# Sharing early-batch work with ScalarE, moving stores to GpSimd, and three smaller schedule edits in a fused attention-and-mixer kernel

## The chip, the cores and the metric

One core of one Trainium2 chip. The metric is device time in microseconds (us) of one execution. TensorE is written PE in the profile, VectorE DVE, ScalarE ACT, GpSimd POOL, SyncE SP. To evacuate a PSUM buffer is to copy its contents to SBUF.

## The reference

Eight batches pass through a linear attention with 8 heads, then through a low-rank mixer and a two-layer network.

```python
q_p = concat(relu(q) * cos_w, relu(q) * sin_w)      # features, 8 x 8 x 576 x 128
k_p = concat(relu(k) * cos_w, relu(k) * sin_w)
kv  = einsum('bhsf,bhsd->bhfd', k_p, v);  z = sum(k_p, axis=2)
x   = (q_p @ kv) / (q_p . z + 1e-6)                 # reordered to 8 x 576 x 512
u   = x + (x^T @ U @ V)^T                           # rank 32
out = u + relu(u @ w_ch1) @ w_ch2                   # 512 -> 2048 -> 512
```

## The kernel before

The 576 rows of a batch are four chunks of 128 rows and a tail of 64. TensorE's order is a list of slots: for each pair of batches 16 slots with the first product of the even batch (`g_ps`, evacuated by ACT as `hid`), 16 of the odd batch, 4 of both tails (`gt_ps`), then 36 slots with a quarter each of a chunk's second product (`o_ps`). The attention of later batches is threaded between those slots by a plan of small units: a kv unit computes half of `kv` and `z`, an x unit one chunk of `x`, the A unit `x^T @ U`, a u unit one chunk of `u`. A k half is the cos or the sin half of one chunk's k features, one call of `scaled_relu`.

```python
def scaled_relu(eng, o, i, w):              # one half (cos or sin) of a feature
    if eng is nc.scalar:
        nc.scalar.activation(out=o, in_=i, func=AF.Relu, bias=0.0, scale=w)
    else:
        eng.tensor_scalar(out=o, in0=i, scalar1=0.0, scalar2=w, op0=ALU.max, op1=ALU.mult)

def g2_part(pr, cc, part):
    if part == 0:
        o_ps[pr, cc] = ps.tile([P, DM], FP32, tag="o", bufs=2, name="o_ps")
    # ... four of the chunk's 16 products, 512 columns each ...
    if part < 3:
        return
    o_sb = pool.tile([P, DM], FP32, tag="o_sb", bufs=3, name="o_sb")
    nc.vector.tensor_tensor(out=o_sb, in0=u, in1=o, op=ALU.add)
    nc.scalar.dma_start(out=..., in_=o_sb)  # the store sits in ACT's in-order queue

def attention_plan(b):                      # offsets in slots from the batch's base
    p0 = -18 if b % 2 == 0 and b > 2 else -14
    plan = [(p0, lambda: v_prep(b))]        # v casts, on GpSimd
    for n, c in enumerate(ORD):             # ORD = (4, 0, 1, 2, 3), 4 is the tail
        plan.append((p0 + n, lambda c=c: k_prep(b, c, (V_, V_))))
        # ... q features on ACT (batch 2: one half on DVE) ...
        plan.append((-9 + 2 * n, lambda c=c: qtr_unit(b, c)))   # q transposes
    # ... kv at 0 and 2; x units at 4, 6, .. 12; A at 14; u at 16 .. 20 ...

for b, w in ((2, 40), (3, 57), (4, 88), (5, 124), (6, 160), (7, 196)):
    ...                                     # the batch's plan at base slot w
```

The transposes, kv, A and u units share one PSUM buffer (tag `T`), the x units another (tag `X`). Both are filled by TensorE and must be emptied by DVE or ACT before they are filled again.

Of the kernel before, what the change touches and what calls it, by code (L numbers as in the profile page):

```python
# [13 lines left out]
ALU = mybir.AluOpType  # L14
# [3 lines left out]
def kernel(  # L18
# [11 lines left out]
    nc = tc.nc  # L30
# [7 lines left out]
    DM = 512  # L38
    DH = 2048
    R = 32  # L40
    NJ = DH // P
    NPAIR = B // 2
# [44 lines left out]
    w2_bf = const.tile([P, NJ, DM], BF16)  # L87
# [13 lines left out]
    def cast(eng, o, i):  # L101
# [6 lines left out]
    V_, A_, G_ = nc.vector, nc.scalar, nc.gpsimd  # L108
# [9 lines left out]
        out=iota[:, 0:4], pattern=[[1, 4]], base=0, channel_multiplier=4,  # L118
        allow_small_or_imprecise_dtypes=True,
    )  # L120
    for lo in (0, TS):
        nc.gpsimd.iota(
            out=iota[lo : lo + TS, 4:5], pattern=[[1, 1]], base=512, channel_multiplier=1,
            allow_small_or_imprecise_dtypes=True,
        )
    for h0 in (0, 4):
# [19 lines left out]
        out=stU[:, 0:4, :], in_=moe_U[0:512, :].rearrange("(p c) r -> p c r", c=4)  # L146
# [23 lines left out]
    def keep_warm(n, tag, bufs):  # L170
        w_ps = ps.tile([P, 512], FP32, tag=tag, bufs=bufs, name="w_ps")
        for _ in range(n):
            nc.tensor.matmul(out=w_ps, lhsT=zero[:, 0:P], rhs=zero, start=True, stop=True)
# [16 lines left out]
    u_bf, u_tl, uT, uT_tl = {}, {}, {}, {}  # L190
# [26 lines left out]
    def k_prep(b, c, engs, h0=0, h1=H):  # L217
        if b not in k_p:
            k_p[b] = pool.tile([P, 4, H, 2 * D], BF16, tag="k_p", bufs=1, name="k_p")
        src = kst[b][:, h0:h1, c, :] if c < 4 else kt[b][:, h0:h1, :]  # L220
        prep(k_p[b][:, c] if c < 4 else k_tl, src, b, c, engs, h0, h1)
# [7 lines left out]
    def kv_unit(b, hg, tag, bufs, eng=None):  # L229
        if b not in kv_sb:  # L230
            kv_sb[b] = pool.tile([P, H, E], BF16, tag="kv", bufs=2, name="kv")
        acc = ps.tile([P, 4, E], FP32, tag=tag, bufs=bufs, name="kv_ps")
        vx = v_ext[b % 2]
        for i in range(4):
            h = hg * 4 + i
            for c in range(5):
                nc.tensor.matmul(  # L237
                    out=acc[:, i, :],
                    lhsT=k_p[b][:, c, h, :] if c < 4 else k_tl[:, h, :],
                    rhs=vx[:, c, h, :],  # L240
                    start=(c == 0),
                    stop=(c == 4),
                )
        cast(eng or V_, kv_sb[b][:, hg * 4 : hg * 4 + 4, :], acc)
# [5 lines left out]
    def qtr_unit(b, c, h0=0, h1=H, eng=None, tag="T", bufs=1):  # L250
        qT_alloc(b)
        t_ps = ps.tile([P, H, P], BF16, tag=tag, bufs=bufs, name="t_ps")
        for h in range(h0, h1):
            nc.tensor.transpose(  # L254
                out=t_ps[:, h, :],
                in_=q_p[b][:, c, h, :] if c < 4 else q_tl[:, h, :],
                identity=ident,
            )
        if c < 4:
            cast(eng or V_, q_pT[b][:, c, h0:h1, :], t_ps[:, h0:h1, :])  # L260
        else:
            cast(eng or V_, q_tlT[:, h0:h1, tail(b)], t_ps[:, h0:h1, tail(b)])
# [161 lines left out]
    hid, hid_tl = {}, {}  # L424
# [37 lines left out]

    def g2_part(pr, cc, part):

        if part == 0:
            o_ps[pr, cc] = ps.tile([P, DM], FP32, tag="o", bufs=2, name="o_ps")
        o = o_ps[pr, cc]
        if cc == 4:
            lhs, c = hid_tl[pr], 0
        else:  # L470
            b, c = (2 * pr, cc) if cc < 4 else (2 * pr + 1, cc - 5)
            lhs = hid[b]
        for j in range(part * 4, part * 4 + 4):
            nc.tensor.matmul(  # L474
                out=o,
                lhsT=lhs[:, j, c * P : c * P + P],
                rhs=w2_bf[:, j, :],
                start=(j == 0),
                stop=(j == NJ - 1),
            )  # L480
        if part < 3:
            return
        o_sb = pool.tile([P, DM], FP32, tag="o_sb", bufs=3, name="o_sb")
        u = u_tl[pr] if cc == 4 else u_bf[b][:, c, :]
        nc.vector.tensor_tensor(out=o_sb, in0=u, in1=o, op=ALU.add)  # L485
        if cc == 4:
            for i in range(2):
                nc.scalar.dma_start(
                    out=out[2 * pr + i, 512:S, :], in_=o_sb[i * TS : i * TS + TS, :]
                )  # L490
        else:
            nc.scalar.dma_start(
                out=out[b, 0:512, :].rearrange("(p c) n -> p c n", c=4)[:, c, :], in_=o_sb
            )


# [18 lines left out]
    ORD = (4, 0, 1, 2, 3)  # L515

    def attention_plan(b):

        p0 = -18 if b % 2 == 0 and b > 2 else -14
        plan = [(p0, lambda: v_prep(b))]  # L520
        for n, c in enumerate(ORD):
            plan.append((p0 + n, lambda c=c: k_prep(b, c, (V_, V_))))
            if b == 2:
                plan.append((p0 + n, lambda c=c: q_prep(b, c, (V_, A_))))
            else:
                plan.append((p0 + n, lambda c=c: q_prep(b, c, (A_, None))))
                plan.append((p0 + n + 1, lambda c=c: q_prep(b, c, (None, A_))))
            plan.append((-9 + 2 * n, lambda c=c: qtr_unit(b, c)))
        plan.append((0, lambda: kv_unit(b, 0, "T", 1)))
        plan.append((2, lambda: kv_unit(b, 1, "T", 1)))  # L530
        for n, c in enumerate(ORD):
            plan.append((4 + 2 * n, lambda c=c: x_unit(b, c, "X", 1)))
        plan.append((14, lambda: A_unit(b, "T", 1)))
        for n, c in enumerate(ORD):
            plan.append((16 + n, lambda c=c: u_unit(b, c, "T", 1)))
        if b % 2 == 1:
            plan.append((18, lambda: utr_dma(b, 4, 5)))
        plan.append((19, lambda: utr_dma(b, 0, 2)))
        plan.append((21, lambda: utr_dma(b, 2, 4)))
        if b + 1 < B:  # L540
            for at, t in zip((p0 + 1, p0 + 2, p0 + 7), loads(b + 1, nc.sync)):
                plan.append((at, t))
        return plan


    l1 = loads(1, nc.sync)
    keep_warm(10, "X", 1)
    for c in ORD:
        k_prep(0, c, (V_, A_), 0, 4)
    l1[0]()  # L550
# [19 lines left out]
    keep_warm(3, "o", 2)  # L570
    for c in ORD[:2]:
        xh_unit(0, c, 0, 4, rec0, "o", 2)
    for n, c in enumerate(ORD):
        qtr_unit(0, c, 4, 8, (A_, A_, V_, A_, V_)[n], "g", 3)
    for c in ORD[2:]:
        xh_unit(0, c, 0, 4, rec0, "o", 2)
    kv_unit(0, 1, "T", 1)
    k_prep(1, 4, (V_, A_))
    uTd_open(0, 0, "g", 3)
    uTd_open(0, 1, "g", 3)  # L580
    rec1 = den_unit(0, 4, 8, "X", 1)
    k_prep(1, 0, (V_, A_))
    a0 = A_unit(0, "T", 1, A_, 0, 256)
    xh_unit(0, 4, 4, 8, rec1, "o", 2)
    xh_unit(0, 0, 4, 8, rec1, "o", 2)
# [2 lines left out]
    uTd_close(0, 1, A_)  # L588
    xh_unit(0, 2, 4, 8, rec1, "o", 2)
    xh_unit(0, 3, 4, 8, rec1, "o", 2)  # L590
    for c in (1, 2, 3):
        k_prep(1, c, (V_ if c == 1 else None, A_))
    uTd_open(0, 2, "g", 3)
    uTd_open(0, 3, "o", 2)
    A_unit(0, "T", 1, V_, 256, 512, a0)
    uTd_close(0, 2, V_)
    uTd_close(0, 3, A_)
    for c in (2, 3):
        k_prep(1, c, (V_, None))
    w1_load(2)  # L600
    v_prep(1, 0, 8, (4, 0, 1))
    w1_load(3)
# [9 lines left out]
    for n, c in enumerate(ORD):  # L612
        at((1, 2, 3, 4, 5)[n], lambda c=c: q_prep(1, c, (V_, A_)))
        ev = A_ if n in (0, 3) else V_
# [16 lines left out]
    for pr in range(NPAIR):  # L631
        e, o = 2 * pr, 2 * pr + 1
# [54 lines left out]
```

## Time and profile before

| | before |
|---|---|
| median of three runs | 356.58 us (356.54 to 357.55) |
| span of the profiled run | 355.6 us |
| PE busy, PE not busy | 327.5 us, 28 us |
| DVE, ACT, POOL busy | 169.1, 143.4, 37.1 us |

The lines that carry the argument stand in the prediction. Here are one group and one row of the DMA table from the page that it only uses in passing. Columns: line, engine, operation, output and input, shapes, count; then total busy us and mean ns of one; then the engine's idle time just before them and what ended most of it. The row below it gives KB of one store and the median us from issue to landing.

```profile
L431 PE MATMUL g_ps<-uT,w_bf 128*128 128x512 bf16 x512 | 121.2, 379 | 2.1 <-ACT hid L438 1.7
...
out_dram<-o_sb ACTq DMA_DIRECT2D x32, 256.0 KB, 2.4
```

TensorE waits for ACT's `hid` in the first product, and a store is in memory 2.4 us after ACT issues it. ACT's timeline (start, duration):

```profile
82.70 5.69 ACTq L492 DMA_DIRECT2D out_dram<-o_sb  x2
88.44 0.72 ACT L203 ACTIVATE q_tl<-qt,cosw 64x512 bf16<-64x512 f32 x1 [10.21 <-DMA out_dram<-o_sb]
```

The queue stood at two store issues for 5.69 us, since the second had to wait for its data. Batch 3's features came after them in the queue.

### The profile page before, as it was taken

How to read it: one execution, taken by the hardware profiler on the slowest of the kernel's cores; microseconds unless marked ns; L12 is line 12 of the kernel's file. 1: busy time of each engine (PE TensorE's matmuls, PEld its weight loads, DVE VectorE, ACT ScalarE, POOL GpSimd, SP SyncE). 2: the span in 40 equal slices, each digit the busy share in tenths (PEclk: the TensorE clock that was granted, in tenths of full speed). 3: DMA queues.
4: the chain of work that ended last, by engine and by line, in shares of the span. 5: the costliest groups of instructions: out<-in, count | busy, mean ns of one | idle time of the engine just before them, and what ended most of it. 6: DMA issues, size and time to landing. Idle time of an engine off the chain costs nothing.

```text
span 355.6 us, 6095 instructions
## 1 busy us (share of the span) xinstructions
PE 327.5 (92%) x2539; PEld 175.7 (49%) x2539; DVE 169.1 (48%) x362; ACT 143.4 (40%) x249; POOL 37.1 (10%) x71
## 2 busy tenths in 40 slices
PE   4669999999787988999999988999999999999995
PEld 1454664475443534556555534556555544464442
DVE  4775454764955685244744681244744640001121
ACT  1957745650600066555530048555530026760000
POOL 6340503030300012000003000300000000000000
PEclk9698999999999999999999999999999999999998
DMA  7999999969242775300896159500312150000221
GB/s 211 259 279 254 196 220 255 259 169 281 80 147 55 189 247 137 58 2 0 125 287 199 59 143 244 147 2 2 89 61 59 61 133 2 1 2 29 88 81 69
DMA packets 60172, 46.04 MB, mean 129 GB/s; under 512 B 26704, under 2 KB 55408, under 8 KB 60144
## 3 DMA queue, kind: packets, MB, share of 16 engines
q1 hardware_dynamic: 50400, 31.46, 36.2%
q0 software_dynamic: 4496, 4.74, 7.9%
q10 hardware_dynamic: 5248, 9.44, 7.7%
q8 instruction: 20, 0.33, 0.4%
q14 instruction: 8, 0.07, 0.1%
HBM read 36.86 MB, written 9.44 MB: 130 GB/s over the span
## 4 chain that ended last, share of the span: by engine, by line
PE 77%; DVE 8%; DMA 8%; ACT 2%; SPq 2%; issue 1%; POOL 1%; POOLq 0%; DVEq 0%; ACTq 0%
PE o_ps L474 31%; PE g_ps L431 28%; DMA kst<-in_k_dram 5%; PE t_ps L254 4%; PE gt_ps L449 4%; DMA vt<-in_v_dram 3%; PE va_ps L361 3%; PE a_ps L344 2%; PE kv_ps L237 2%; PE x_ps L318 2%; DVE k_p L205 2%; ACT q_p L203 1%; DVE o_sb L485 1%; SPq L75 1%; DVE u_bf L362 1%
## 5 line engine op out<-in xcount | busy, mean ns | idle before, releaser
L431 PE MATMUL g_ps<-uT,w_bf 128*128 128x512 bf16 x512 | 121.2, 379 | 2.1 <-ACT hid L438 1.7
L474 PE MATMUL o_ps<-w_bf,hid 128*128 128x512 bf16 x512 | 119.3, 379 | 0.0
L438 ACT ACTIVATE hid<-g_ps 128x512 bf16<-128x512 f32 x128 | 75.9, 596 | 77.8 <-PE g_ps L431 77.6
L431 PEld LDWEIGHTS <-w_bf 128*128 128x128 bf16 x512 | 48.0, 98 | 59.5 <-issue 10.1
L474 PEld LDWEIGHTS <-hid 128*128 128x128 bf16 x512 | 48.0, 98 | 52.2 <-issue 1.2
L485 DVE TENSOR_TENSOR o_sb<-u_bf,o_ps 128x512 f32<-128x512 bf16 x32 | 21.9, 684 | 61.9 <-PE o_ps L474 61.9
L105 POOL CAST v_ext<-vst 128x512 bf16<-128x512 f32 (+1 forms) x32 | 18.3, 610 | 169.1 <-DMA vst<-in_v_dram 140.8
L105 DVE COPY q_pT<-t_ps 128x1024 bf16<-128x1024 bf16 (+1 forms) x29 | 19.4, 671 | 30.0 <-PE t_ps L254 28.6
L203 ACT ACTIVATE q_tl<-qt,cosw 64x512 bf16<-64x512 f32 x5 | 3.6, 719 | 62.0 <-DVE rec L276 27.3
L362 DVE TENSOR_TENSOR u_bf<-x_bf,va_ps 128x512 bf16<-128x512 bf16 x32 | 21.9, 685 | 12.1 <-PE va_ps L361 12.0
L254 PE MATMUL t_ps<-ident,q_p 128*128 128x128 bf16 x256 | 20.6, 224 | 4.1 <-ACT q_tlT L103 1.0
L203 ACT ACTIVATE q_p<-qst,sinw 128x512 bf16<-128x512 f32 (+1 forms) x36 | 23.3, 664 | 2.4 <-DVE o_sb L485 2.3
L254 PEld LDWEIGHTS <-q_p 128*128 128x128 bf16 x256 | 17.4, 100 | 10.8 <-issue 5.0
L205 DVE TENSOR_SCALAR k_p<-kst,cosw 128x512 bf16<-128x512 f32 (+1 forms) x36 | 16.8, 482 | 2.8 <-DMA kst<-in_k_dram 2.7
L361 PE MATMUL va_ps<-A_sb,V_bf 128*128 128x512 bf16 x40 | 15.1, 377 | 2.8 <-DVE u_bf L362 2.4
L328 DVE TENSOR_TENSOR x_bf<-x_ps,rec 128x512 bf16<-128x512 f32 x24 | 16.6, 691 | 0.8
L449 PE MATMUL gt_ps<-uT_tl,w_bf 128*128 128x128 bf16 x256 | 16.1, 219 | 0.0
L449 PEld LDWEIGHTS <-w_bf 128*128 128x128 bf16 x256 | 15.1, 98 | 1.4
L474 PE MATMUL o_ps<-w_bf,hid_tl 128*128 128x512 bf16 x64 | 15.4, 379 | 0.0
L105 DVE CAST kv<-kv_ps 128x260 bf16<-128x260 f32 x16 | 6.9, 429 | 17.2 <-PE kv_ps L237 17.2
L237 PEld LDWEIGHTS <-k_p 128*128 128x128 bf16 x256 | 11.1, 99 | 7.8 <-DVE q_pT L105 2.5
L237 PE MATMUL kv_ps<-v_ext,k_p 128*128 128x65 bf16 x256 | 12.3, 195 | 2.5 <-DVE u_bf L362 1.9
(93 smaller groups left out, 254.0 us busy)
## 6 DMA issues: line engine op xcount, KB each, us to landing
out_dram<-o_sb ACTq DMA_DIRECT2D x32, 256.0 KB, 2.4
kst<-in_k_dram SPq DMA_DIRECT2D x7, 1024.0 KB, 11.2
qst<-in_q_dram SPq DMA_DIRECT2D x7, 1024.0 KB, 7.9
vst<-in_v_dram SPq DMA_DIRECT2D x7, 1024.0 KB, 11.1
w_bf<-in_moe_w_ch_dram POOLq DMA_DIRECT2D x8, 512.0 KB, 12.0
kst<-in_k_dram SPq DMA_DIRECT2D x2, 512.0 KB, 7.8
qst<-in_q_dram SPq DMA_DIRECT2D x2, 512.0 KB, 8.7
vst<-in_v_dram SPq DMA_DIRECT2D x2, 512.0 KB, 11.4
```

What stands on the lines that cost most here:

```text
L105: eng.tensor_copy(out=o, in_=i)
L203: nc.scalar.activation(out=o, in_=i, func=AF.Relu, bias=0.0, scale=w)
L205: eng.tensor_scalar(out=o, in0=i, scalar1=0.0, scalar2=w, op0=ALU.max, op1=ALU.mult)
L237: nc.tensor.matmul(out=acc[:, i, :], lhsT=k_p[b][:, c, h, :] if c < 4 else k_tl[:, h, :], rhs=vx[:, c, h, :], start=(c == 0), stop=(c == 4),)
L254: nc.tensor.transpose(out=t_ps[:, h, :], in_=q_p[b][:, c, h, :] if c < 4 else q_tl[:, h, :], identity=ident,)
L361: nc.tensor.matmul(out=va, lhsT=V_bf[:, c, :], rhs=A_sb[b], start=True, stop=True)
L362: nc.vector.tensor_tensor(out=u_bf[b][:, c, :] if c < 4 else u_tl[b // 2][rows, :], in0=x_of(b, c, rows), in1=va[rows, :], op=ALU.add,)
L431: nc.tensor.matmul(out=g_ps.rearrange("p (c t) -> p c t", c=4), lhsT=w1_bf[:, d, j * P : j * P + P], rhs=uT[b][:, :, d, :], start=(d == 0) ...
L438: nc.scalar.activation(out=hid[b][:, j, :], in_=g_ps, func=AF.Relu, bias=0.0, scale=1.0)
L449: nc.tensor.matmul(out=g_ps[:, jj, :], lhsT=w1_bf[:, d, j * P : j * P + P], rhs=uT_tl[pr][:, d, :], start=(d == 0), stop=(d == 3),)
L474: nc.tensor.matmul(out=o, lhsT=lhs[:, j, c * P : c * P + P], rhs=w2_bf[:, j, :], start=(j == 0), stop=(j == NJ - 1),)
L485: nc.vector.tensor_tensor(out=o_sb, in0=u, in1=o, op=ALU.add)
```

## The change

Five intents: work of batches 2 and 3 goes from DVE to ACT; the stores leave ACT's queue for GpSimd's (the last pair's go to SyncE's), so that ACT is free for that work; the features of batches 4 and 6 move eight slots earlier, out of the slots of the first product; the start is reordered so that batch 1's k features don't hold up batch 0's chain; the last chunk is computed in two column halves. In the core of the diff, cuts are marked:

```diff
 def g2_part(pr, cc, part):
+    last = pr == NPAIR - 1 and cc == 8
     ...
+    if last:      # first 256 columns, all 16 products; then the other 256
+        cols, js = slice(part // 2 * 256, part // 2 * 256 + 256), part % 2 * 8
+        js = range(js, js + 8)
     ...
-    nc.vector.tensor_tensor(out=o_sb, in0=u, in1=o, op=ALU.add)
+    nc.vector.tensor_tensor(out=o_sb[:, cols], in0=u[:, cols], in1=o[:, cols], op=ALU.add)
+    eng = nc.sync if pr == NPAIR - 1 else nc.gpsimd
-    nc.scalar.dma_start(...)
+    eng.dma_start(...)

 def attention_plan(b):
-    p0 = -18 if b % 2 == 0 and b > 2 else -14
+    p0 = -26 if b % 2 == 0 and b > 2 else -14
     for n, c in enumerate(ORD):
-        plan.append((p0 + n, lambda c=c: k_prep(b, c, (V_, V_))))
+        ke = (V_, A_) if b == 3 else (V_, V_)
+        plan.append((p0 + n, lambda c=c, ke=ke: k_prep(b, c, ke)))
     ...
-        plan.append((-9 + 2 * n, lambda c=c: qtr_unit(b, c)))
+        ev = A_ if b in (2, 3) and n % 2 == 0 else V_
+        plan.append((-9 + 2 * n, lambda c=c, ev=ev: qtr_unit(b, c, eng=ev)))

 # the start
-keep_warm(10, "X", 1)
+keep_warm(20, "X", 1)
 ...
+kv_unit(0, 1, "T", 1)          # between the third and fourth q transpose,
 ...                            # before: after the last x unit of the first half
-k_prep(1, 4, (V_, A_)); ...; k_prep(1, 0, (V_, A_))   # between uT, den and A of batch 0
 ...
+k_prep(1, 4, (None, A_)); k_prep(1, 0, (None, A_))    # only after batch 0's x units
 ...                            # and the other halves after its last uT
```

More of the change, by code (lines that the diff above doesn't have):

```diff
@@ L468, in g2_part @@
         if cc == 4:
-            lhs, c = hid_tl[pr], 0
+            b, lhs, c, u = None, hid_tl[pr], 0, u_tl[pr]
         else:
             b, c = (2 * pr, cc) if cc < 4 else (2 * pr + 1, cc - 5)
-            lhs = hid[b]
-        for j in range(part * 4, part * 4 + 4):
+            lhs, u = hid[b], u_bf[b][:, c, :]
+        if last:
+            cols, js = slice(part // 2 * 256, part // 2 * 256 + 256), part % 2 * 8
+            js = range(js, js + 8)
+        else:
+            cols, js = slice(0, DM), range(part * 4, part * 4 + 4)
+        for j in js:
             nc.tensor.matmul(
-                out=o,
+                out=o[:, cols],
                 lhsT=lhs[:, j, c * P : c * P + P],
-                rhs=w2_bf[:, j, :],
+                rhs=w2_bf[:, j, cols],
                 start=(j == 0),
@@ L480, in g2_part @@
             )
-        if part < 3:
+        if js[-1] < NJ - 1:
             return
         o_sb = pool.tile([P, DM], FP32, tag="o_sb", bufs=3, name="o_sb")
-        u = u_tl[pr] if cc == 4 else u_bf[b][:, c, :]
-        nc.vector.tensor_tensor(out=o_sb, in0=u, in1=o, op=ALU.add)
+        nc.vector.tensor_tensor(
+            out=o_sb[:, cols], in0=u[:, cols], in1=o[:, cols], op=ALU.add
+        )
+        eng = nc.sync if pr == NPAIR - 1 else nc.gpsimd
         if cc == 4:
             for i in range(2):
-                nc.scalar.dma_start(
+                eng.dma_start(
                     out=out[2 * pr + i, 512:S, :], in_=o_sb[i * TS : i * TS + TS, :]
@@ L491, in g2_part @@
         else:
-            nc.scalar.dma_start(
-                out=out[b, 0:512, :].rearrange("(p c) n -> p c n", c=4)[:, c, :], in_=o_sb
+            eng.dma_start(
+                out=out[b, 0:512, cols].rearrange("(p c) n -> p c n", c=4)[:, c, :],
+                in_=o_sb[:, cols],
             )
@@ L572 @@
         xh_unit(0, c, 0, 4, rec0, "o", 2)
-    for n, c in enumerate(ORD):
-        qtr_unit(0, c, 4, 8, (A_, A_, V_, A_, V_)[n], "g", 3)
+    for n, c in enumerate(ORD[:3]):
+        qtr_unit(0, c, 4, 8, (A_, A_, V_)[n], "g", 3)
+    kv_unit(0, 1, "T", 1)
+    for n, c in enumerate(ORD[3:]):
+        qtr_unit(0, c, 4, 8, (A_, V_)[n], "g", 3)
     for c in ORD[2:]:
         xh_unit(0, c, 0, 4, rec0, "o", 2)
-    kv_unit(0, 1, "T", 1)
-    k_prep(1, 4, (V_, A_))
     uTd_open(0, 0, "g", 3)
@@ L581 @@
     rec1 = den_unit(0, 4, 8, "X", 1)
-    k_prep(1, 0, (V_, A_))
     a0 = A_unit(0, "T", 1, A_, 0, 256)
@@ L590 @@
     xh_unit(0, 3, 4, 8, rec1, "o", 2)
-    for c in (1, 2, 3):
-        k_prep(1, c, (V_ if c == 1 else None, A_))
+    k_prep(1, 4, (None, A_))
+    k_prep(1, 0, (None, A_))
     uTd_open(0, 2, "g", 3)
@@ L597 @@
     uTd_close(0, 3, A_)
-    for c in (2, 3):
-        k_prep(1, c, (V_, None))
+    for c in ORD:
+        k_prep(1, c, (V_, None if c in (4, 0) else V_))
     w1_load(2)
```

## The prediction

> **What bounds the kernel now.** I read the engine shares first, then the chain that ended last, then ten-microsecond windows to see where TensorE is not full, then the timeline inside those windows.
>
> ```profile
> PE 327.5 (92%) x2539; PEld 175.7 (49%) x2539; DVE 169.1 (48%) x362; ACT 143.4 (40%) x249; POOL 37.1 (10%) x71
> ...
> PE 77%; DVE 8%; DMA 8%; ACT 2%; SPq 2%; issue 1%; POOL 1%; POOLq 0%; DVEq 0%; ACTq 0%
> ```
>
> TensorE is the bound, and no other engine is half full. No product is removed, so the change can win only from TensorE's gaps: 355.6 - 327.5 = 28 us. The windows say where these are (columns after the stretch: PE, PEld, DVE, ACT, POOL busy; then clock and DMA).
>
> ```profile
> core 0: us, PE busy (x) PEld busy (x) DVE busy (x) ACT busy (x) POOL busy (x), PEclk, DMA share, GB/s
> 0.00:10.00 10.00, 4.37 (x10) 1.34 (x10) 5.06 (x19) 2.81 (x6) 5.37 (x16) 0.94 0.81 206
> 10.00:20.00 10.00, 7.58 (x95) 5.74 (x96) 7.40 (x25) 10.00 (x26) 5.52 (x13) 0.72 1.12 281
> 20.00:30.00 10.00, 7.01 (x104) 5.16 (x102) 6.03 (x16) 5.22 (x9) 2.10 (x5) 0.83 1.18 249
> ...
> 90.00:100.00 10.00, 7.82 (x73) 4.25 (x73) 8.24 (x21) 4.91 (x8) 3.33 (x5) 1.00 0.28 85
> 100.00:110.00 10.00, 7.78 (x51) 3.87 (x50) 6.18 (x12) 0.00 (x0) 0.00 (x0) 1.00 0.37 118
> 110.00:120.00 10.00, 8.35 (x86) 4.67 (x87) 5.70 (x12) 0.00 (x0) 0.00 (x0) 1.00 0.37 79
> ...
> 130.00:140.00 10.00, 8.21 (x43) 3.71 (x42) 7.12 (x12) 8.36 (x15) 3.41 (x5) 1.00 0.35 79
> ...
> 210.00:220.00 10.00, 8.15 (x41) 3.65 (x41) 4.19 (x10) 9.40 (x17) 0.00 (x0) 1.00 1.06 255
> ```
>
> Idle TensorE: 11.0 us before 30 us, 6.05 us from 90 to 120 (ACT is empty from 100 to 120), 1.8 near 130, 1.85 near 210. The timeline names the releaser of each gap.
>
> ```profile
> 24.56 0.72 ACT L203 ACTIVATE k_p<-kst,sinw 128x512 bf16<-128x512 f32 x1 [1.83 <-DMA kst<-in_k_dram]
> ...
> 24.95 0.41 DVE L304 TENSOR_TENSOR x_tl<-xh_ps,rec 64x256 bf16<-64x256 f32 x1
> 25.19 0.36 ACT L103 ACTIVATE A_sb<-a_ps 128x256 bf16<-128x256 f32 x1
> ...
> 25.61 0.42 PE L402 MATMUL uT_ps<-V_bf,A_sb 128*128 128x512 bf16 x1 [1.65 <-ACT A_sb L103]
> ...
> 75.20 0.61 PE L254 MATMUL t_ps<-ident,q_p 128*128 128x128 bf16 x8 [0.80 <-DVE q_tlT L105]
> ...
> 96.77 0.43 PE L318 MATMUL x_ps<-kv,q_pT 128*128 128x65 bf16 x8 [1.40 <-DVE x_bf L328]
> ...
> 100.47 0.61 PE L254 MATMUL t_ps<-ident,q_p 128*128 128x128 bf16 x8 [0.78 <-DVE q_pT L105]
> ...
> 133.54 0.38 PE L361 MATMUL va_ps<-A_sb,V_bf 128*128 128x512 bf16 x1 [0.75 <-DVE u_bf L362]
> ...
> 215.09 1.02 PE L431 MATMUL g_ps<-uT,w_bf 128*128 128x512 bf16 x4 [0.68 <-ACT hid L438]
> ```
>
> Batch 1's k features sit in the in-order queues of ACT and DVE ahead of batch 0's evacuations, and its load lands only at 24.6. So x_tl and A_sb are late, and TensorE waits. Later the releaser is a backlog on DVE (75.20, 96.77, 133.54) or on ACT (215.09). A part of the gaps is different: at 100.47, 104.71, 108.03 and 110.57 TensorE waits 0.77 to 0.78 us, just one evacuation of 0.69 us plus some 0.1. There one PSUM buffer is filled, emptied and filled again with nothing between; a free engine doesn't shorten that.
>
> **What the Trainium skill says.** "ScalarE: Activation LUTs", section "What ACT_TABLE_LOAD costs": an ACTIVATE takes 186 ns + 0.833 ns an element with immediate operands, about 93 ns more for a pointer scale. The trace agrees: 596 ns for hid (512 elements), 710 for a q feature (pointer scale), 1.04 us for a q_pT copy of 1024. DVE copies q_pT in 0.69 us, so ACT is the slower evacuator.
> "VectorE: DVE Perf Modes", section "The perf-mode tier table (the rule you actually need)": an fp32 SBUF tensor_scalar runs at twice the basic rate, a tensor_tensor from PSUM at the basic one. The trace: 0.47 us for a k feature of 512 (0.395 from start to start), 0.69 for x_bf, u_bf and o_sb.
> "DMA: Bandwidth & Descriptors", section "SWDGE vs HWDGE vs iDMA": a DMA issued from GpSimd has its descriptors written in software. The trace has weight loads on POOL at 746 to 912 ns an issue, against 0.34 us for a store on ACT that finds its data ready. POOL is 90% idle.
> "TensorE: Matmul & The Clock Gate", section "What's actually happening": an idle window of some 3.4 us throttles the array to half rate, some 3.4 us of work releases it. The trace: after the idle stretch 5.56 to 11.43 us eight transposes take 0.86 us, later 0.44; after the gap ending 25.61 eight of them again spread over some 0.9.
>
> **The change part by part.**
>
> *Start.* (a) Ten more warm-up products: 10 x 0.43 = 4.3 us from 5.56, over at 9.9, before the first transpose at 11.43. They delay nothing; the first transposes run at full rate. But ACT is full from 10 to 20, so little of that arrives: -0.2. (b) Batch 1's k features leave the queue ahead of batch 0's chain. The second kv product moves up into a 0.59 us TensorE wait at 18.9 to 19.5. By hand along DVE: rec at 23.9 as now, x_tl then at once, at 23.95 instead of 24.95: -1.0. A_sb follows at 24.0 instead of 25.19, so the gap before 25.61 nearly closes and the array stays warm: eight transposes (0.86 to 0.44) and four half-width A products (0.86 to 0.5) save 0.8. First g product 28.5 instead of 30.48. (c) Does it stay? Batch 1's q lands at 32.5, which still allows the interleaved slots to begin 2 us earlier; v lands at 38.6, and the kv product moves from 41.6 to 39.7; the last quarter of w1 lands at 45.45, while its first use moves from 47.35 to 45.4. All three just hold. The start gives **-2.0**.
>
> *Batches 2 and 3.* q_tlT of batch 2 goes to ACT, so the 0.80 at 75.20 goes: **-0.8**. For batch 3, five k halves of 0.395 (2.0 us) and three evacuations (0.41 + 2 x 0.69 = 1.8 us) leave DVE, which is 82% busy from 90 to 100. Its backlog gaps 0.46 (92.76) and 1.40 (96.77) are 1.86; I leave 0.3. The structural 0.78s stay. On ACT the last evacuation is 1.04 instead of 0.69 ahead of a u product only four matmuls away: +0.35. Together 1.86 - 0.3 - 0.35 = **-1.2**. ACT carries it: without the stores ahead of them, batch 3's features start near 84 when their buffers are free (now 88.44, held 10.21 us behind a store), 15 x 0.62 = 9.3 us.
>
> *Features of batches 4 and 6 eight slots earlier*, out of the first product's slots, where ACT also evacuates hid: gaps of 0.35 + 0.75 + 0.69 = 1.8 for batch 4, and 0.74 + 0.37 + 0.68 + 0.68 = 2.5 for batch 6 vanish. But in the instruction order of the changed kernel the ten k halves now stand between the x_bf evacuations of the batch before. For batch 4: two slots are 1.98 us of TensorE; DVE must do in them one x unit (1.03), four k halves (1.58) and half an o_sb (0.30), 2.9. With one PSUM buffer for x, TensorE waits; stepping through the five slots I get 0.1 + 0.65 + 1.2 = 1.95. For batch 6 only the last two x units are concerned: 0.85 + 0.33 + 0.12 = 1.3. Net 4.3 - 3.25 = **-1.0**.
>
> *Stores on GpSimd:* 30 issues of about 0.75 us on an idle engine, hidden; they free ACT. *End:* now o_sb runs 351.55 to 352.24 and the span ends 3.3 us later. With halves the last add is some 0.41 instead of 0.69 (the 256-column x_bf takes 0.41), half of the 256 KB is out before, and 32 products of 256 columns cost perhaps 0.1 more than 16 of 512: **-0.4**.
>
> Sum: -2.0 - 0.8 - 1.2 - 1.0 - 0.4 = -5.4; 356.58 - 5.4 = **351.2 us**.
>
> **The rivals.**
> 1. *The moved features only move the stall.* For: the 2.9 against 1.98 us above. If GpSimd's v casts fall on the same time, k halves stretch as at 93 us now (0.83 to 0.92 against 0.47), ten of them by up to 0.4. Then batches 4 and 6 gain nothing or lose 1 to 2: 353 us.
> 2. *The start is bound by loads.* For: DMA is saturated (1.1 to 1.2) from 10 to 60 us. The last w1 quarter is issued on POOL behind batch 1's v casts, so its landing doesn't move up with TensorE. If a landing slips by 1 us, so does the gain: 352.5. Against: the three margins fit now, if barely.
> 3. *The store issue becomes the wait.* A store on GpSimd waits behind a v cast whose load is late; three output buffers fill, DVE waits, TensorE follows. For: v casts waited 140 us for loads. Against: in the new order each v load is issued well ahead of its cast. It would make 354 to 356.
> 4. *Fewer backlogs than I count.* If DVE has slack at batches 4 and 6 because k features spread into later slots, both gaps go: 349 us.
>
> **Range and chances.** The five terms are uncertain by about 0.8, 0.3, 0.7, 1.5 and 0.3 us, together near 1.9. Rivals 1 to 3 pull up, 4 pulls down. I take 349.0 to 353.8. Two per cent faster means below about 349.5: 17%. Within 2%: 82%. Slower by 2%: 1%, as no new work is on TensorE.
>
> **What would show it.** First g product near 28.5 us, with x_tl near 24; if it starts there but the first tail product (72.45 now) hasn't moved by 2 us, rival 2. No DVE-released gap of 1.4 between 90 and 98, but still three or four of 0.78 up to 115. No gaps with u_bf or hid as releaser in the first product of batches 2 and 4, and new ones, released by x_bf, in the second product before them (some 1.9 and 1.2 us); none there means rival 4, more means rival 1. POOL with about 30 issues near 0.75 us, and no wait of DVE for a store. I'd be wrong at the root if TensorE's total idle time fell by less than 2 us or by more than 8.

## The result, and the profile after

The kernel is correct. In the runs made together on one chip the changed kernel took 352.17 us (median of four, 352.06 to 352.83) and the kernel before 357.05 (median of four, 356.54 to 357.55). The ratio is 0.9867, with a 95% interval of 0.9845 to 0.989. A ratio here is the mean time of one kernel's fast runs over that of the other's of the same rounds, so not quite the ratio of the medians. This is a gain clear of the noise, but short of two per cent. 351.2 us had been predicted, with a range from 349.0 to 353.8. The span of the profiled run went from 355.6 to 350.3 us. The mean granted clock of the two profiles differs (0.983 and 0.994), but from 30 us on to the end of the work it is 1.00 in both; before that it is 0.83 and 0.94, which is a part of the start.

The changed kernel's page, with the same parts as shown of before: shares of the span, the chain, groups, landings.

```profile
PE 326.5 (93%) x2537; PEld 177.0 (51%) x2565; DVE 165.8 (47%) x355; ACT 150.5 (43%) x257; POOL 52.2 (15%) x101
...
PE 75%; DVE 9%; DMA 9%; issue 3%; POOL 2%; ACT 1%; SPq 0%; POOLq 0%; DVEq 0%
...
L431 PE MATMUL g_ps<-uT,w_bf 128*128 128x512 bf16 x512 | 120.6, 379 | 0.4
L491 DVE TENSOR_TENSOR o_sb<-u_bf,o_ps 128x512 f32<-128x512 bf16 (+1 forms) x33 | 22.1, 669 | 61.6 <-PE o_ps L481 61.6
L501 POOL DMA_DIRECT2D out_dram<-o_sb x24 | 13.4, 558 | 180.9 <-DVE o_sb L491 164.4
...
out_dram<-o_sb POOLq DMA_DIRECT2D x24, 256.0 KB, 4.5
out_dram<-o_sb SPq DMA_DIRECT2D x7, 256.0 KB, 2.3
```

TensorE's work is the same; 28 us of it not busy have become 24. The first product has almost no idle time left (2.1 to 0.4 us). A store issue costs GpSimd 0.56 us. It lands after 4.5 us instead of 2.4, but that is not the price of GpSimd alone: the experiments below give 3.0 with the stores alone on GpSimd and 3.0 with them back on ACT, and from 245 to 286 us, where few loads run, it is 2.4 here against 2.1 before. Nothing waits for it: all idle time of DVE before `o_sb` was ended by TensorE, none by a store.

Four windows of the changed kernel, ten microseconds each, with the columns that the prediction explains (the stretch, its length, then busy PE):

```profile
120.00:130.00 10.00, 8.94 (x55) 4.12 (x55) 6.63 (x15) 1.79 (x3) 2.67 (x5) 1.00 1.12 310
130.00:140.00 10.00, 10.00 (x65) 5.15 (x64) 3.89 (x7) 5.38 (x9) 1.32 (x3) 1.00 0.50 85
...
200.00:210.00 10.00, 8.83 (x40) 3.79 (x40) 6.47 (x12) 1.81 (x4) 3.85 (x7) 1.00 1.15 286
210.00:220.00 10.00, 10.00 (x69) 5.41 (x68) 1.81 (x3) 6.00 (x11) 0.13 (x1) 1.00 0.17 45
```

The holes that the prediction showed at 130 and 210 us are full, but there are new ones just before them. In the kernel before, the stretches just before were fuller:

```profile
120.00:130.00 10.00, 10.00 (x69) 4.76 (x67) 7.71 (x21) 2.17 (x4) 0.00 (x0) 1.00 0.98 305
...
200.00:210.00 10.00, 9.31 (x49) 4.06 (x46) 6.50 (x14) 0.90 (x2) 0.00 (x0) 1.00 0.28 81
```

**Where the 5.3 us are.** TensorE's products come in the same order in both kernels after the start. So I took the start of one and the same product in both traces, slot by slot (of its weight load, since some products are missing in the traces). Where the difference stays constant, nothing is won or lost; where it steps, the step is the gain or the loss of that place. The table's steps add up to the difference of the spans, -5.27 us.

| stretch | predicted | read in the two traces |
|---|---|---|
| start, up to the 13th first product of batch 0 | -2.0 | -3.37 at the first one, -2.66 left at the 13th |
| batch 2's `q_tlT` on ACT | -0.8 | -0.97 |
| rest of batches 2 and 3 | -1.2 | -0.56 |
| features of batch 4 eight slots earlier | +0.15 (1.95 - 1.8) | +0.17 (2.21 - 2.04) |
| features of batch 6 eight slots earlier | -1.2 (1.3 - 2.5) | -1.5 (1.47 - 2.97) |
| end | -0.4 | +0.25 |
| sum | -5.4 (rounded) | -5.27 |

These are three of TensorE's waits in the changed kernel's timeline (start, duration, work; in brackets the idle time before it and its releaser):

```profile
89.85 0.43 PE L318 MATMUL x_ps<-kv,q_pT 128*128 128x65 bf16 x8 [1.16 <-DVE x_bf L328]
...
123.18 0.43 PE L318 MATMUL x_ps<-kv,q_pT 128*128 128x65 bf16 x8 [1.06 <-DVE x_bf L328]
...
344.80 1.91 PE L481 MATMUL o_ps<-w_bf,hid 128*128 128x256 bf16 x16 [0.51 <-DVE o_sb L491]
```

The wait of 1.06 is the foreseen one of batch 4's features (with 0.18 and 0.46 before it). Those at 89.85 and 344.80 were not foreseen. For the first, GpSimd's and then DVE's timeline of the changed kernel show the cause:

```profile
84.87 0.56 POOL L501 DMA_DIRECT2D out_dram<-o_sb  x1 [4.96 <-DVE o_sb L491]
85.43 2.28 POOL L105 CAST v_ext<-vst 128x512 bf16<-128x512 f32 x4
```

```profile
86.16 2.60 DVE L205 TENSOR_SCALAR k_p<-kst,cosw 128x512 bf16<-128x512 f32 x2
```

Two k halves took 2.60 us. Four v casts of batch 3 ran on GpSimd at that time; in the queue they stand behind a store, which had waited 4.96 us for `o_sb`. In "SBUF — State Buffer", section "Who interferes with whom", the Trainium skill says that VectorE in a two-port mode and GpSimd share one pair of ports, and that whichever issues first blocks the other for its whole instruction. The trace agrees that they block each other: the same two halves take 0.86 us in a kernel where the casts lie elsewhere (the early-cast experiment below). The wait can be longer than one instruction, as the run with the stores alone will show. So the store's new place moved the casts onto the k features.

For the wait at 344.80: the two halves of the last chunk are columns of one PSUM tile, and the second half's products waited until DVE had read the first half. In "PSUM — Partial Sum Buffer", section "PSUM bank collisions raise a hardware error ⚠️", the skill says that two engines may not touch one bank at the same time, not even in disjoint columns, so this wait had to be expected. It cost 0.94 us up to the last load of weights (the wait of 0.51 and the narrower products), and the tail after it is only 0.69 us shorter.

### The profile page after: what moved, and what is told of

It is laid out like the page before. It is cut to its first block, busy times and chain, and to the rows that moved or that the text cites. A ratio compares the mean times of both kernels' runs of the same rounds, so it can differ in the third digit from the quotient of the medians.

```text
span 350.3 us, 6126 instructions
## 1 busy us (share of the span) xinstructions
PE 326.5 (93%) x2537; PEld 177.0 (51%) x2565; DVE 165.8 (47%) x355; ACT 150.5 (43%) x257; POOL 52.2 (15%) x101
## 4 chain that ended last, share of the span: by engine, by line
PE 75%; DVE 9%; DMA 9%; issue 3%; POOL 2%; ACT 1%; SPq 0%; POOLq 0%; DVEq 0%
PE o_ps L481 29%; PE g_ps L431 28%; DMA vst<-in_v_dram 5%; PE gt_ps L449 4%; PE t_ps L254 4%; PE va_ps L361 3%; DMA vt<-in_v_dram 3%; DVE k_p L205 3%; PE kv_ps L237 2%; DVE o_sb L491 2%; PE x_ps L318 2%; PE a_ps L344 2%; DMA w_bf<-in_moe_w_ch_dram 2%; POOL v_ext L105 1%; DVE u_bf L362 1%
## 5 line engine op out<-in xcount | busy, mean ns | idle before, releaser
L481 PE MATMUL o_ps<-w_bf,hid 128*128 128x512 bf16 (+1 forms) x510 | 116.9, 372 | 1.4 <-DVE o_sb L491 0.5
L481 PEld LDWEIGHTS <-hid 128*128 128x128 bf16 x528 | 49.5, 98 | 52.6 <-issue 2.8
L491 DVE TENSOR_TENSOR o_sb<-u_bf,o_ps 128x512 f32<-128x512 bf16 (+1 forms) x33 | 22.1, 669 | 61.6 <-PE o_ps L481 61.6
L501 POOL DMA_DIRECT2D out_dram<-o_sb x24 | 13.4, 558 | 180.9 <-DVE o_sb L491 164.4
L105 DVE COPY q_pT<-t_ps 128x1024 bf16<-128x1024 bf16 (+1 forms) x25 | 16.7, 668 | 26.5 <-PE t_ps L254 24.9
L105 POOL CAST v_ext<-vst 128x512 bf16<-128x512 f32 (+1 forms) x32 | 17.3, 582 | 17.7 <-DMA vst<-in_v_dram 16.1
L205 DVE TENSOR_SCALAR k_p<-kst,cosw 128x512 bf16<-128x512 f32 (+1 forms) x36 | 17.9, 514 | 1.6 <-DMA kst<-in_k_dram 1.6
L203 ACT ACTIVATE q_p<-qst,cosw 128x512 bf16<-128x512 f32 x20 | 14.2, 710 | 2.4 <-DMA qst<-in_q_dram 2.4
```

What stands on the lines that cost most here:

```text
L105: eng.tensor_copy(out=o, in_=i)
L481: nc.tensor.matmul(out=o[:, cols], lhsT=lhs[:, j, c * P : c * P + P], rhs=w2_bf[:, j, cols], start=(j == 0), stop=(j == NJ - 1),)
L491: nc.vector.tensor_tensor(out=o_sb[:, cols], in0=u[:, cols], in1=o[:, cols], op=ALU.add)
```

## The experiments

Three theories stood at first. **Mine:** each part carries the gain that the table gives it, so taking one away costs just that. **Rival 1:** moving the features only moves the stall. **Rival 2:** the start's lead depends on when loads land and does not last.

One difficulty was the noise of the start. The same code starts its first `g_ps` product (its weight load; the product follows 0.2 us later) anywhere between 26.89 and 29.18 us over the eleven profiles with the new start, and between 28.08 and 30.26 over three with the old one. The traces show what goes along with it: ACT's and DVE's first features wait for the tail rows of batch 0's k, whose load GpSimd issues. Here is ACT in the changed kernel, with the earliest start, and in the run `vcast_and_dve`, with the latest:

```profile
7.93 0.51 ACT L203 ACTIVATE k_tl<-kt,sinw 64x256 bf16<-64x256 f32 x1 [5.51 <-DMA kt<-in_k_dram]
9.47 0.51 ACT L203 ACTIVATE k_tl<-kt,sinw 64x256 bf16<-64x256 f32 x1 [7.04 <-DMA kt<-in_k_dram]
```

With the new start this load landed by 7.82 us in six profiles, and the first product came at 26.89 to 27.73; it landed at 9.02 to 9.36 in four, with 28.63 to 29.18; and at 8.40 in one, with 27.40. The granted clock does not sort them: over the first 30 us it is 0.94 in both of the extremes.

After about 48 us the runs built on the changed kernel repeat: where their code is the same, their slots agree within 0.03 us. The kernel before repeats less well: its trace and that of the run with the new start alone differ by 0.35 us near 93 us and by 0.33 near 133, though the code there is the same. So each experiment has two measurements: its time against the kernel before of the same call, and the steps slot by slot after the start, against the changed kernel (or against the kernel before, where that was the base). The second one is the sharper. The changed kernel itself was not timed again in these calls.

**The end in one piece.**

```diff
-    last = pr == NPAIR - 1 and cc == 8
+    last = False
```

> The changed kernel with the last chunk undivided again, as in the kernel before. Theory: the two halves share one PSUM buffer, so the second half's products wait 0.5 us for the first half's addition, and 32 products of 256 columns are no cheaper than 16 of 512; the division costs what it gains or a little more. Expects the same to 0.3 us faster than the changed kernel, 351.9 to 352.2. Rival (the prediction's own step): dividing gains 0.4 us, so this run is at 352.6.

Measured: 353.43 us (352.43 to 354.61), ratio 0.9933 (0.9904 to 0.9962), span 350.7. In the slots, the last weight load came 0.94 us earlier relative to the rest and the tail after it was 1.11 us longer (5.07 against 3.96). Dividing the chunk gains 0.2 us, which no timing here can tell from nothing; the tail of an undivided chunk alone is 4.65 to 5.09 us in the four traces that have one. What the two halves save after the last product is lost before it.

**The features of batches 4 and 6 where they had been.**

```diff
-    p0 = -26 if b % 2 == 0 and b > 2 else -14
+    p0 = {4: -18, 6: -18}.get(b, -14)
```

> The changed kernel with the features of batches 4 and 6 back at their old place, inside the first product. Theory: moving them only exchanges the stalls of batch 4 (about 0) and gains 1.2 to 1.5 for batch 6, so this run is 1.2 to 1.7 us slower than the changed kernel: 353.4 to 353.9. Rival 1: the move gains nothing at all, 352.2 or below. Rival 4: the stalls simply vanished with the move, 4.3 us: 356.

Measured: 352.38 us (351.83 to 353.3), ratio 0.9908 (0.9881 to 0.9936), span 351.5, with a start that was 1.7 us later at the 13th first product. In batch 4's stretch, the x waits go (-2.21) and waits in the first product come back (+1.45). In batch 6's, -1.46 goes and +1.77 comes back. Sum: -0.45 us for the features in their old slots. So the move doesn't gain; it costs a little. At batch 6, this is the wait for ACT that TensorE has here:

```profile
212.51 2.12 PE L431 MATMUL g_ps<-uT,w_bf 128*128 128x512 bf16 x8 [0.64 <-ACT hid L438]
```

With it there is one of 0.95 for DVE. The kernel before, with the features in the same slots, had four waits here of 2.5 us in all. Of the changes made since, the one that touches ACT's queue there is the stores' move. The gain that I had credited to the moved features would then belong to the stores, which the run with the stores alone tests. My theory falls in this part; rival 1 was right.

**The stores back on ACT, all else changed.**

```diff
-    eng = nc.sync if pr == NPAIR - 1 else nc.gpsimd
+    eng = nc.sync if pr == NPAIR - 1 else nc.scalar
```

> The changed kernel with the stores of the first six batches back on ScalarE's queue, those of the last pair still on SyncE. Theory: in the new order ScalarE is not late anywhere with its features, and GpSimd, freed of the stores, does batch 3's v casts some 10 us earlier, away from the k features that they stretch now; so no slower, 351.5 to 352.3, with the wait of x_ps near 89.85 (1.16 us) gone. Rival: taking the stores off ScalarE is a part of the gain, because features and evacuations on it wait behind stores: 353 to 354, with ScalarE's evacuations as releasers of TensorE's waits.

Measured: 357.62 us (355.13 to 362.91, one of the six runs slow), ratio 1.0042 (0.9996 to 1.0088), span 355.9. The whole gain is gone, and what came is the rival of my expectation, only larger. After the start the slots give +5.2 us up to the last weight load (4.8 to the end, since the tail is shorter here). ACT's timeline in this run shows how:

```profile
80.33 1.02 ACT L103 ACTIVATE q_pT<-t_ps 128x1024 bf16<-128x1024 bf16 x1 [3.98 <-DVE o_sb L491]
86.14 0.34 ACTq L501 DMA_DIRECT2D out_dram<-o_sb  x1
86.58 0.72 ACT L203 ACTIVATE k_tl<-kt,sinw 64x512 bf16<-64x512 f32 x1 [5.23 <-PE x_ps L318]
```

TensorE's, a little later:

```profile
95.92 0.91 PE L254 MATMUL t_ps<-ident,q_p 128*128 128x128 bf16 x8 [2.67 <-ACT q_tlT L103]
```

An evacuation that TensorE needs stands behind a store that waits for its data, and the features start at 86.58 instead of 83.04 (0.82 us of this is the later start). The evacuation of `q_tlT` behind those features is late by 2.67 us. The 1.16 us wait at x is gone here, as GpSimd's casts run earlier with no store ahead of them. Still, the store's place is the condition of the sharing. I had given it no term of its own.

**The start as it had been.** The edit takes back the last hunk of the diff.

```diff
-keep_warm(20, "X", 1)
+keep_warm(10, "X", 1)
 ... kv_unit(0, 1) and all k_prep(1, ...) at their places of before
```

> The changed kernel with the whole start (up to the first g product) as in the kernel before: 10 warm-up products, batch 1's k features ahead of batch 0's evacuations. Theory: the start is worth 2.0 to 2.7 us of the 4.9: 354.2 to 354.9, the first g product back near 30 us, and the later stretches unchanged. Rival (loads bind, the lead of the start is given back): 352.7 or less.

Measured: 353.22 us (352.58 to 354.69), ratio 0.9934 (0.9906 to 0.9963), span 351.1. The first `g_ps` product came at 28.40, 1.5 us later than in the changed kernel's profile; 0.87 of that was left at the 13th, and later slots were the same. That is less than half of the 2.0 predicted, and the run is faster than I had expected, nearer to its rival. The time can't be told from that of the kernel with the undivided end of the same call.

**Only the stores.** The base is the kernel before; the stores of the first six batches are on GpSimd, the last pair's on ACT.

```diff
-    nc.scalar.dma_start(
+    (nc.scalar if pr == NPAIR - 1 else nc.gpsimd).dma_start(
```

> The kernel BEFORE with one part of the change alone: the stores of the first six batches issued from GpSimd instead of ScalarE. Theory: ScalarE is no longer held behind stores and does the q features of batches 4 and 6 ahead of the first product, so of the 2.0 and 3.0 us that the kernel before loses there about 0.6 and 1.2 return; the v casts behind the stores stretch batch 3's k features and take some 0.5 back. Net 1 to 1.5 us faster than before, ratio 0.996 to 0.997. Rival A (the stores by themselves are the large part of the gain): ratio 0.99 or below. Rival B (the stores only matter together with the work shared to ScalarE): ratio 0.999 to 1.002.

Measured: 357.25 us (355.72 to 358.09), ratio 1.003 (0.9992 to 1.0067), span 353.9. That span profits from an early start (first `g_ps` at 28.08 against 30.26). After the start, the slots against the kernel before give +2.49 at batch 3, -0.79 after it, -0.66 at batch 4 and -1.2 at batch 6: -0.16 in all. In this run, TensorE's wait and DVE's k half:

```profile
90.63 0.43 PE L318 MATMUL x_ps<-kv,q_pT 128*128 128x65 bf16 x8 [2.49 <-DVE x_tl L328]
```

```profile
86.46 2.98 DVE L205 TENSOR_SCALAR k_tl<-kt,sinw 64x512 bf16<-64x512 f32 x1
```

So the stores' move alone gains 0.66 and 1.2 us at batches 4 and 6, with the features in their old slots; the kernel with the whole change but these slots stands at -0.59 (0.17 - 0.76) and -1.2 (-1.5 + 0.31) there. The two agree: the gain is the stores'. (Against the run with the new start alone, which has the same code there, batch 4's is 0.98 and not 0.66, so it is known to 0.3 only.) The move gives it back at batch 3, where the v casts behind a store hold up a single k half for 2.98 us. That half, from 86.46 to 89.44, spans the end of a store's issue and all four casts, of 0.62 us each: so it seems not to have been let in between them. My expectation of a gain of 1 to 1.5 us was wrong; rival B is the nearest. In the runs made here, stores and sharing gain only together.

**Batches 2 and 3 on DVE again, all else changed.**

```diff
-            ke = (V_, A_) if b == 3 else (V_, V_)
+            ke = (V_, V_)
-            ev = A_ if b in (2, 3) and n % 2 == 0 else V_
+            ev = V_
```

> The changed kernel with the sharing of batches 2 and 3 undone: all their evacuations and both halves of batch 3's k features on VectorE again. Theory: the 0.8 us stall before the second tail product returns, and the waits of x_ps for x_bf between 85 and 100 grow from 1.2 to 2.5 us or more, since the k features also meet the v casts: 2.0 to 2.5 us slower than the changed kernel, 354.2 to 354.7. Rival (sharing only swaps engines): within 0.5 us of the changed kernel.

Measured: 356.97 us (355.89 to 357.21), ratio 1.0021 (0.9991 to 1.0051), span 355.1. The slots give +0.95 at batch 2 and +2.5 at batch 3, in all 3.4 us. Both waits are back in TensorE's timeline:

```profile
73.92 0.61 PE L254 MATMUL t_ps<-ident,q_p 128*128 128x128 bf16 x8 [0.80 <-DVE q_tlT L105]
91.35 0.43 PE L318 MATMUL x_ps<-kv,q_pT 128*128 128x65 bf16 x8 [2.49 <-DVE x_tl L328]
```

The direction was as expected and the size larger: with stores on GpSimd, the second wait isn't the 1.40 of before, but the 2.49 of the run with the stores alone.

**The sine halves of batches 4 and 6 on ACT too.** If the new x waits come from ten k halves between the x evacuations on DVE, ACT should take five of them.

```diff
-            ke = (V_, A_) if b == 3 else (V_, V_)
+            ke = (V_, A_) if b in (3, 4, 6) else (V_, V_)
```

> The changed kernel with the sin halves of the k features of batches 4 and 6 on ScalarE too, as the change does for batch 3. Theory: VectorE's ten k halves between the x evacuations cost 2.2 us at batch 4 and 1.5 at batch 6; with five of them on the idle ScalarE at most 0.4 of each is left: 2.0 to 3.0 us faster than the changed kernel, 349.2 to 350.2. Rival (the waits there come of the single x buffer and not of the k halves): no more than 0.5 us faster.

Measured: 348.85 us (348.53 to 349.22), ratio 0.98 (0.9769 to 0.9831), span 347.0. The slots give -0.35, -0.64 and -0.95 at batch 4 and -0.51 and -0.95 at batch 6: -3.4 us. All waits on `x_bf` are gone there; this is the only one that TensorE has left between 195 and 215 us:

```profile
203.65 0.38 PE L361 MATMUL va_ps<-A_sb,V_bf 128*128 128x512 bf16 x1 [0.22 <-DVE u_bf L362]
```

The cause holds: DVE's backlog made these waits. Whether the sharing would have paid with the features in their old slots too was not run.

**Batch 3's v casts earlier**, in slot 38 instead of 43, so that they are done before the k features start.

```diff
-        plan = [(p0, lambda: v_prep(b))]
+        plan = [(38 - 57 if b == 3 else p0, lambda: v_prep(b))]
```

> The changed kernel with GpSimd's v casts of batch 3 put ahead of the first two stores in GpSimd's queue, so that they run when the load lands, some ten us earlier. Theory: the first two k features of batch 3, which take 2.6 us together in the changed kernel instead of 0.9, are stretched by these casts, and so the wait of x_ps for x_bf of 1.16 us goes: 0.6 to 1.0 us faster, 351.2 to 351.6. Rival (the stretch has another cause, such as ScalarE's reads of the same tiles): no change, and the two features still 2 us or more.

Measured: 352.57 us (351.78 to 353.08), ratio 0.9901 (0.9872 to 0.993), span 350.0. DVE's k halves, then TensorE's next wait:

```profile
86.08 0.86 DVE L205 TENSOR_SCALAR k_p<-kst,cosw 128x512 bf16<-128x512 f32 x2
```

```profile
92.30 0.61 PE L254 MATMUL t_ps<-ident,q_p 128*128 128x128 bf16 x8 [1.00 <-ACT q_tlT L103]
```

The two halves fell from 2.60 to 0.86 us and the wait of 1.16 is gone: -1.34 in the slots. But +1.16 comes back two slots on, where TensorE now waits for ACT. The cause is shown; the gain that I had expected (0.6 to 1.0 us) went into the next engine's backlog.

**The same, with batch 3's `q_tlT` back on DVE.**

```diff
-            ev = A_ if b in (2, 3) and n % 2 == 0 else V_
+            ev = A_ if (b, n) in ((2, 0), (2, 2), (2, 4), (3, 2), (3, 4)) else V_
```

> The changed kernel with batch 3's v casts ahead of the stores, as in the run before, and in addition batch 3's first evacuation (q_tlT) back on VectorE. Theory: with the casts early the 1.16 us wait for x_bf went, but ScalarE, with 15 features in its queue, was 1.0 us late with q_tlT; with VectorE, now less held up, doing it, both waits go: 1.0 to 1.4 us less between the second x unit of batch 2 and its last than in the changed kernel, 350.9 to 351.4. Rival: VectorE is then late itself, and the net stays within 0.3 us.

Measured: 351.26 us (350.64 to 352.66), ratio 0.9866 (0.9839 to 0.9893), span 350.8 with a first `g_ps` product 2.29 us later than in the changed kernel's profile. The slots keep -1.34, and nothing comes back. So ACT's evacuation was the wait that had taken over.

**Only the start.** The kernel before with the new start section, and nothing else of the change.

```diff
-keep_warm(10, "X", 1)
+keep_warm(20, "X", 1)
 ... kv_unit(0, 1) and all k_prep(1, ...) at their places of the change
```

> The kernel BEFORE with the new start alone (20 warm-up products, second kv product and batch 0's evacuations ahead of batch 1's k features). Profiles of the same start differ by up to 2 us, since the loads land differently. From the timed runs of the two calls before, less each kernel's fixed time after the 14th g product, the new start is ahead by 0.5 to 0.8 us there, and by 2.1 on the chip of the prediction. Theory: the first g product is 1 to 2 us earlier, but the g product that first needs the last quarter of w1 then begins within 0.3 us of its landing, so only 0.4 to 1.2 us stay: ratio 0.9965 to 0.999. Rival (the whole 2.0 of the prediction stays): 0.9945 or below.

Measured: 355.74 us (355.21 to 356.96), ratio 0.9988 (0.9963 to 1.0013), span 353.8. Against the profile of before, the lead is 3.1 us at the first `g_ps` product, 2.51 at the 11th, 2.14 in the second product and 1.79 at the end. The timed gain is 0.4 us, with an interval from a gain of 1.3 to a loss of 0.5. The profile of before had drawn a late start, and 0.7 us of the lead is given back after the start, in the two steps near 93 and 133 us; I have not traced why.

**The last quarter of w1 issued between the v casts**, to see whether its landing holds the 13th product.

```diff
-    v_prep(1, 0, 8, (4, 0, 1))
+    v_prep(1, 0, 8, (4,))
     w1_load(3)
+    v_prep(1, 0, 8, (0, 1))
```

> The changed kernel with the load of the last w1 quarter issued from GpSimd some 4 us earlier, between batch 1's v casts. Theory: the loads saturate the DMA engines there, so an earlier issue only takes the share of v's load: w1's quarter lands 2 to 4 us earlier and no longer binds, v lands 0.5 to 1.5 us later and delays batch 1's kv product; net between 0.3 us faster and 0.8 slower. Rival (the issue behind the casts is what binds): 0.3 to 0.8 us faster, with v landing as before.

Measured: 353.09 us (351.87 to 354.04), ratio 0.9909 (0.9881 to 0.9937), span 351.9. The quarter landed at 43.32 instead of 44.62, but this run's start was 1.74 us late, so the product came at 46.30 and didn't need it early. Inconclusive: it doesn't show whether an early landing helps an early start.

**All that helped, put together**: sine halves on ACT for batches 3, 4 and 6; the early casts; of batch 3's evacuations only one on ACT; the last chunk's halves in two PSUM buffers.

```diff
+        if last and part == 2:
+            o_ps[pr, cc] = ps.tile([P, DM], FP32, tag="g", bufs=3, name="o2_ps")
-        plan = [(p0, lambda: v_prep(b))]
+        plan = [(38 - 57 if b == 3 else p0, lambda: v_prep(b))]
-            ke = (V_, A_) if b == 3 else (V_, V_)
+            ke = (V_, A_) if b in (3, 4, 6) else (V_, V_)
-            ev = A_ if b in (2, 3) and n % 2 == 0 else V_
+            ev = A_ if (b, n) in ((2, 0), (2, 2), (3, 2)) else V_
```

> A version meant to beat both: the changed kernel with the sin halves of batches 4 and 6 on ScalarE, batch 3's v casts ahead of the stores, only the three evacuations on ScalarE that nothing follows closely (batch 2's first and third, batch 3's third), and the last chunk's halves in two PSUM buffers. Theory: 3.4 from the k halves, 1.2 from the casts and q_tlT, 0.2 + 0.25 from the two late evacuations, 0.5 from the second buffer: 5.0 to 5.7 us faster than the changed kernel, 346.5 to 347.2, ratio 0.972 to 0.976. Each term is to be seen by itself as a gap gone. Rival: with one gap closed the next engine is late, and less than 4 us come.

Measured: 347.19 us (346.25 to 348.06), ratio 0.9747 (0.9718 to 0.9777), span 344.6: 2.5% faster than the kernel before. Its shares, and DVE's timeline at the end:

```profile
PE 325.9 (95%) x2537; PEld 177.5 (51%) x2565; DVE 161.6 (47%) x348; ACT 154.0 (45%) x264; POOL 51.8 (15%) x101
```

```profile
339.36 0.42 DVE L493 TENSOR_TENSOR o_sb<-u_bf,o_ps 128x256 f32<-128x256 bf16 x1 [1.06 <-PE o_ps L483]
341.11 0.42 DVE L493 TENSOR_TENSOR o_sb<-u_bf,o_ps 128x256 f32<-128x256 bf16 x1 [1.32 <-PE o_ps L483]
```

1.75 us lie between the two last additions; the changed kernel's were at 344.32 and 346.74, 2.42 apart. The wait of 0.51 us is gone. Between 90 and 115 us, five waits of 0.77 to 1.08 us are left, where one PSUM buffer is filled, emptied and filled again.

## Why the prediction was right

The time fell within the range and 1 us from the value, but not each term is right. In the order of its own steps:

- **What bounds it: right.** TensorE's work did not change, and its idle time fell by some 4 us.
- **Start, -2.0 with the three loads that "all just hold": right in the pair of profiles, too large elsewhere.** `x_tl` of the second half came at 22.92 and the first `g_ps` product at 27.10, earlier than predicted; the first tail product moved from 72.45 to 69.78, so most of the lead was kept. But the 13th product's weight load started only when the last w1 quarter had landed (44.62); this cost 0.24 us of the 0.7 by which the lead shrank on the way. Rival 2 is partly right. Step (a), booked at 0.2 us, failed: the warm-up products were over at 7.41 and not at 9.9, TensorE stood idle for 3.47 us, and from 12 to 14 us its granted clock was 0.50, so the first transposes did not run at full rate. In step (b), the eight transposes after 25.61 that I read as 0.9 us are 1.3, with two waits among them.
  Other runs give a second estimate. In eight of them the start is the new one and the step after it is known. Taking those steps out of the measured ratios, each as its share of the time, puts the changed kernel at 0.990 to 0.993 of the kernel before on those three chips, on the average 0.991, which is 3.2 us. The slots after the start account for 2.6 of that (5.27 - 2.66), which leaves about 0.6 us for the start, with intervals of the single ratios near 1 us either way. The two experiments on the start itself say 0.9 (by slots) and 0.4 (by time). On the first chip, the timed difference was 4.7 us by the ratio, which leaves 2.1.
  So the pair of profiles was lucky. The tail rows of batch 0's k landed at 7.82 us in the changed kernel's and at 8.76 in that of before. That one also had batch 1's k late (24.45, against 23.51 and 22.04 in the other two with the old start) and a half clock from 26 to 29 us, where the other two had 1.00. Where the tail rows land at 8.4 to 9.1 us, the new start's first product comes at 27.40 to 29.06 and the old one's at 28.08 to 30.26. No run sets a landing, so how much of the lead it makes is not shown.
- **Batch 2, -0.8: right** (-0.97).
- **Batch 3, -1.2: mis-sized, -0.56.** The mechanism was right: the 1.40 wait went, and a late ACT evacuation cost 0.33 of the 0.35 allowed. Another 0.18 came from batch 2's last evacuation, for which nothing had been allowed. The term that failed is "I leave 0.3" for DVE's backlog. The v casts, moved behind a store, blocked two k halves, and 1.16 us of wait came instead. I had foreseen this collision for batches 4 and 6 only.
- **Batches 4 and 6, -1.0 net: right as a sum** (-1.33), each as stepped through (+0.17 and -1.5). But the cause was wrong: with the features left in their old slots, the sum is 0.45 us better still, and the stores alone bring -0.66 and -1.2 there. The prediction booked 4.3 us of vanishing waits as the features' gain. 5.0 vanished, and 3.2 of them came back with the features in their old slots: the other 1.8 had gone with the stores, and the 3.2 are less than the 3.7 of new waits. At batch 6 the larger new wait was also not the one foreseen: 0.87 us for `u_tl`, with 0.34 for `x_bf`. Rival 4 did not come.
- **Stores, "hidden; they free ACT": right, but not priced.** They are the condition of the sharing: without them the change loses 5.2 us, and alone they bring 0.2, as batch 3 gives back what batches 4 and 6 gain. An issue cost 0.56 us instead of 0.75. Rival 3 did not come: no DVE wait for a store.
- **End, -0.4: wrong sign in the profile, +0.25** (a gain of 0.2 against the undivided end in the changed kernel). The step left out was that the second half waits for the first one's reader.

That the sum came so near is in part luck. The overestimates at batch 3 and at the end, 1.3 us together, were made up for by the start in that pair of profiles (0.7) and by batches 2 and 6. A prediction that is right in its sum is not yet right in its terms; only the runs that undo or isolate a part have told that.

## What to carry to other kernels

An issue of a store in an in-order queue blocks what stands behind it until its data is ready, so move stores off an engine before giving it work that another engine waits for, and look at what the store then blocks in the queue it moves to. Moving work away from a stall only pays if the place it moves to has room: here the same features gained nothing by the move, and the kernel gained 3.4 us once half of their k part went to another engine. When one engine's wait goes, look at the next few products for the engine that takes its place, as with the 1.16 us that turned into 1.00 us on ACT.

## What the Trainium skill lacked or had wrong

- "DMA: Bandwidth & Descriptors", section "Anatomy of one DMA — SWDGE (gpsimd) path", has a fit for a whole DMA from GpSimd, 2.0 us plus the bytes at 436 GB/s; for 256 KB the estimate from it is 2.6 us. A store landed 2.4 us after its issue where few loads ran, so that holds. What it lacks is how much other traffic adds: the median of all 24 is 4.5 us, the longest 8.3. It has no figure either for what an issue costs GpSimd itself: 0.56 us.
- The same page says that a DMA's wait for a semaphore happens on the issuing sequencer, but not that this stops the compute behind it. Here ACT's queue stood for 5.69 us at two stores, and with the stores put back 3.98 us passed before an evacuation.
- "SBUF — State Buffer", section "Who interferes with whom", gives the shared ports to whichever issues first, for its whole instruction. Here the blocked one seems to have waited for a whole run of instructions: one k half took 2.98 us across four casts of 0.62, and two took 2.60 beside such casts and 0.86 without them.
- No page that I read names the landing of the first loads as a source of noise. The start differs by 2.3 us between executions of the same code (first `g_ps` product at 26.89 to 29.18 us), against 0.4 us that the new start alone gained in the timed runs, with a granted clock of 0.94 over the first 30 us in both extremes. "TensorE: Matmul & The Clock Gate" warns of such a variation for the clock only.
- "PSUM — Partial Sum Buffer" has the rule for which the program makes the second column half of one tile wait, but gives no time for such a wait: 0.51 us here, and none with two buffers.
